# Softmax denominators of an attention and SwiGLU kernel: the reciprocal taken of 14 columns between two 32x32 block transposes, in place of 448 columns

## The chip, the core and the metric

The kernel runs on one core of one Trainium2 chip. A core has five engines that run side by side, each through its own list of instructions in order: TensorE (PE in the profile) for matmuls, VectorE (DVE), ScalarE (ACT), GpSimd (POOL), and SyncE (SP), whose queue issues the DMAs here. They wait for one another through semaphores. The time is device time in microseconds (us) of one launch. Before the change it is 1558.87 us, the median of 3 runs (1558.22 to 1562.27).

## The reference

The program is an attention block followed by a gated feed-forward block, all in float32.

- Attention, for 8 batches x 12 heads, 448 positions, head dimension 64: `q` and `k` are RMS-normalised along the head dimension and multiplied by gains; `scores = q k^T / 8`; `attn = exp(scores - max)`; `attn = attn / (sum(attn) + 1e-9)`; output `attn v`.
- The heads are put side by side to rows `x` of 8*448 = 3584 tokens x 768.
- Feed-forward: `x` is RMS-normalised and multiplied by a gain; `g = x w_gate`, `val = x w_val` (768 to 1536); `out = (g * sigmoid(g) * val) w_out` (1536 to 768).

The sum of `attn` over the keys is the softmax denominator; there is one for every batch, head and query position. Its reciprocal is what the change is about.

## The kernel before

**Tiling.** Attention works on pairs of heads: `NG` = 48 pairs `g`, six (`NPAIR`) for each of 8 sequences `b`. The scores of a pair are computed transposed, keys on the partitions and the 448 queries along the free axis, so `exp` (tile `e`, by ScalarE, lines 566 and 656) needs no transposing before it is multiplied by `v`. The value product of a pair is gathered in a PSUM bank `av` of 128 x 448: 64 rows for the head dimension of one head, 64 for the other. There is only one buffer of that kind (`ps_m`, tag "m"), which the transposes of q and k share; a new `av`, or such a transpose, waits until the last one was read. No maximum is subtracted: a bound on the gains is computed (line 1555), and a second routine, `any_scores`, takes over where it fails; with these inputs it isn't run.

**The denominators.** TensorE also multiplies `exp` by a matrix of ones 64 columns wide, so the sum over the keys lands in *all* 64 rows of a head: `den`, 128 x 448 in PSUM, has 64 equal rows for one head and 64 equal rows for the other. This saves a broadcast later. There are two ways to it:

- The first 7 pairs: `sums(g)` (line 592) sums with 12 matmuls (line 598), takes the reciprocal straight from PSUM into `rd` (line 601), and calls `weigh`.
- The other 41 pairs: GpSimd first adds the seven `e` tiles (`later_sums`, lines 701 and 706). Every second pair, `totals(g)` (line 676) takes two pairs at once: it sums with the ones (line 684), ScalarE copies the banks to `rd` (lines 688 and 691), VectorE takes the reciprocal in place (line 693) and `weigh` follows.

`weigh(g, ...)` (line 625) multiplies `av`, or a copy of it already in `x`, by `rd` on VectorE (line 630). Some steps later ScalarE squares the result (line 635, into the buffer of `rd`) and GpSimd adds the squares to `ss` (line 636), from which, once in a sequence, the RMS factor of the feed-forward is made (`rms_x`, line 713, and `norm_x`, line 724).

**Feed-forward.** Sequence 0 uses plain matmuls (line 1432), the others Strassen-like products (`quad`, line 1078, matmuls on line 1073; second projection on lines 1297 and 1365), whose sums VectorE makes. The feed-forward of a sequence is cut into items in a list `todo`; `fill` (line 1466) puts as many of them between the attention steps of the next sequence as their costs say.

**Weights.** The weights come as float64. `convert()` (line 872) turns them to float32 in 72 pieces, each over several turns: DMA in (line 821), two ScalarE passes (lines 834 and 835), three VectorE passes (`join`, lines 840, 841 and 842), and an integer add on GpSimd (line 882); then the piece is stored for later sequences (line 870). This goes on until about 285 us.

**Order.** The whole order of each engine's list is written out by hand: `manual_schedule` for all five engines, with `pe(fn)` as the step counter and `after(n, fn)` to put the rest of a job n steps later. So no engine can pass a waiting instruction: what stands behind it in its own list waits too. The pool `tmp`, which holds `rd` in two buffers, lies in SBUF.

Of the kernel before, what the change touches and what calls it, by code (L numbers as in the profile page):

```python
# [8 lines left out]
F32 = mybir.dt.float32  # L9
# [9 lines left out]
B, H, S, D = 8, 12, 448, 64  # L19
# [316 lines left out]
def safe_scores(  # L336
# [20 lines left out]
    nc = tc.nc  # L357

    def pool(name, bufs, **kw):
        return ctx.enter_context(tc.tile_pool(name=name, bufs=bufs, **kw))  # L360
# [4 lines left out]
    e_pool, tmp, y_pool, rest_pool = pool("c_e", 11), pool("c_tmp", 1), pool("c_y", 3), pool("c_rest", 2)  # L365
# [8 lines left out]
    st = {}  # L374
# [24 lines left out]
    def own(j):  # L399
        return slice(j * D, (j + 1) * D)  # L400

    def across(j):
        return own(1 - j)
# [180 lines left out]
    def values(g):  # L584

        vt, av = st["v", g], st["av", g]
        for c in range(NK):
            for j in range(2):
                nc.tensor.matmul(av[own(j), 0:S], lhsT=vt[:, j, c], rhs=st["e", g, c, j], start=False,
                                 stop=(c == NK - 1), skip_group_check=True)  # L590

    def sums(g):


        den = st.pop(("den", g))
        for c in range(NK):
            for j in range(2):
                nc.tensor.matmul(den[own(j), 0:S], lhsT=ones, rhs=st["e", g, c, j], start=False, stop=c == NK - 1,
                                 skip_group_check=True)
        rd = st["rd", g] = tmp.tile([128, S], F32, name="rd", tag="rd", bufs=2)  # L600
        nc.vector.reciprocal(rd, den[:, 0:S])
        weigh(g, *((1, 1) if g == NPAIR - 1 else (3,)))

    def x_of(g):
# [20 lines left out]
    def weigh(g, n, m=None):  # L625

        b, hp = divmod(g, NPAIR)
        rd, x = st.pop(("rd", g)), x_of(g)
        held = ("av", g) not in st
        nc.vector.tensor_tensor(x, x if held else st.pop(("av", g))[:, 0:S], rd, ALU.mult)  # L630
        ss, m = st["ss", b], n + 1 if m is None else m
        if hp == 0:
            after(n, lambda: nc.scalar.activation(ss, x, ACT.Square))
        else:
            after(n, lambda: nc.scalar.activation(rd, x, ACT.Square))  # L635
            after(m, lambda: (nc.gpsimd.tensor_tensor(ss, ss, rd, ALU.add), st.update({("summed", b): hp})))  # L636
        if not held:
            close(g)
# [37 lines left out]
    def totals(g):  # L676

        which = (g, g - 1) if g > NPAIR + 1 else (g,)
        den = {i: ps_s.tile([128, 512], F32, name="den", tag="s") for i in which[::-1]}
        for i in which:  # L680
            es = st.pop(("es", i))
            for j in range(2):
                to = j if i == g else 1 - j
                nc.tensor.matmul(den[i][own(to), 0:S], lhsT=ones[across(j)], rhs=es[across(j)], start=True, stop=True)  # L684
        for i in which[::-1]:
            rd = st["rd", i] = tmp.tile([128, S], F32, name="rd", tag="rd", bufs=2)
            if i == g:
                nc.scalar.copy(rd, den[i][:, 0:S])
            else:
                for j in range(2):  # L690
                    nc.scalar.copy(rd[own(j)], den[i][across(j), 0:S])  # L691
        for i in which[::-1]:
            nc.vector.reciprocal(st["rd", i], st["rd", i])  # L693
            if i < g:
                weigh(i, 3, 4)

# [381 lines left out]
    def quad(b, fp):  # L1078
# [72 lines left out]
        def p3_last():  # L1151
            if fp == NFP - 1 and in_quads(b):
                after(1, lambda: left_q1(b, 0, range(3)))
            p3()
            if fp % KG == KG - 1:
                after(3, lambda: sums(0))
                after(3 if fp == NFP - 1 else 5, lambda: sums(1))
# [434 lines left out]
    for g in range(NG + 1):  # L1592
# [24 lines left out]
        if g <= NPAIR:  # L1617
            pe(lambda: score(g, (0,)))
            squares(g + 2, 0)
            squares(g + 2, 1)  # L1620
            if g > 1:
                pe(lambda: turn(g + 1, 0))
                some_rests(g)
                pe(lambda: turn(g + 1, 1))
            pe(lambda: rests(g))
            pe(lambda: values(g - 1))
            if g == 1:
                pe(lambda: turn(g + 1, 0))
                some_rests(g)
                pe(lambda: turn(g + 1, 1))  # L1630
            load_v(g + 2)

            turns(1 if g == 1 else 3 if g < NPAIR else 0)
            pe(lambda: sums(g - 1))
            pe(lambda: score(g, (1, 2)))
            turns(2 if g == 1 else 3 if g == NPAIR else 0)
            if g == 2:
                bound()
            if g == NPAIR - 1:
                for half in range(2):  # L1640
                    norm_k(g + 2, half)
            continue

        if g == NPAIR + 1:
            some = lambda *parts: [exps(g, i, scores(g, i)) for i in parts]
            pe(lambda: (rests(g), some(0, 1)))
            pe(lambda: rms_x(0))
            pe(lambda: values(g - 1))
            load_v(g + 2)
            pe(lambda: some(2, 3))  # L1650
            pe(lambda: norm_x(0))
            pe(lambda: some(4, 5))
            pe(lambda: sums(g - 1))
            later_sums(g, 2)
            begin(0, 15)
        else:
            sums_due = g % 2 == 0
            pe(lambda: (totals(g - 1) if sums_due else None, step(g, 0)))
            pe(lambda: [step(g, i) for i in (1, 2)])
            load_v(g + 2)  # L1660
            pe(lambda: [step(g, i) for i in (3, 4)])
            pe(lambda: ([step(g, i) for i in (5, 6)], weigh(g - 1, 2) if sums_due else hold(g - 1)))
            if g < NG:
                later_sums(g, 2)
# [32 lines left out]
@with_exitstack  # L1697
def kernel(ctx: ExitStack, tc: tile.TileContext, *args):
    nc = tc.nc
    flag = ctx.enter_context(tc.tile_pool(name="flag", bufs=1)).tile([1, 1], I32, name="flag")  # L1700
    safe_scores(tc, *args, flag)
    large = nc.values_load(flag[0:1, 0:1], min_val=0, max_val=1)
    with tc.If(large > 0):
        any_scores(tc, *args)
# [28 lines left out]
```

## Time and profile before

| | before |
|---|---|
| median of 3 runs | 1558.87 us |
| the profiled execution | 1557.32 us |
| its span, first to last instruction | 1555.5 us |
| ScalarE busy | 535.3 us, 34% |
| GpSimd busy | 734.3 us, 47% |
| all DMA | 327 MB, mean 210 GB/s |
| mean granted TensorE clock | 0.994 |

How to read it: the profile is of one execution, whose time is 1.8 us more than its span. A row of a group names line, engine, operation, tiles written and read, partitions x elements, and the count; then total busy time, the mean of one in ns, and the idle time of the engine ahead of it. A row of the timeline gives start, length, engine, line, operation, tiles and count, and in brackets the engine's idle time ahead and what ended it. TensorE's matmuls are pipelined and their ends are modelled, so it counts as busy even where it gets through less than it could.

### The profile page before, as it was taken

Reading aid. Unit: us, or ns where it says so; the run is one execution under the profiler, and the core shown is the slowest. Engines: PE = TensorE matmul, PEld = TensorE weight load, DVE = VectorE, ACT = ScalarE, POOL = GpSimd, SP = SyncE. Lnnn points to the kernel's source line nnn. Section 1 sums busy time; section 2 is a strip of 40 time slices with the busy share of each in tenths; the row PEclk is TensorE's granted clock in tenths of the full one; section 3 lists DMA queues with packets and bytes.
Section 4 is the critical chain, followed back from the end, with each engine's and each line's share of the span. In section 5 each row is a group of like instructions: output and inputs, shape, how many; then the busy total and the mean of one; then the engine's idle time right before and its main releaser. Section 6 shows DMA issues by size and latency. Waiting matters only on the chain.

```text
span 1555.5 us, 25996 instructions
## 1 busy us (share of the span) xinstructions
PE 1515.4 (97%) x8900; PEld 1187.2 (76%) x8900; DVE 1009.3 (65%) x1697; ACT 535.3 (34%) x1241; POOL 734.3 (47%) x718
## 2 busy tenths in 40 slices
PE   8999998999999999999999999999999999999997
PEld 4344444687855888878987889768888789899997
DVE  6889989668864677855468564643568554673454
ACT  6756654433323333233333242333432332101000
POOL 6868877556433354463535644444544732021003
PEclk9999999999999999999999999999999999999999
DMA  7657565676889987986557765485557755578665
GB/s 205 210 154 242 185 207 164 208 237 213 285 268 288 316 259 230 281 257 187 166 157 229 236 196 165 139 260 161 159 148 234 227 172 147 156 263 255 174 195 180
DMA packets 314081, 327.26 MB, mean 210 GB/s; under 512 B 84308, under 2 KB 310868, under 8 KB 313940
## 3 DMA queue, kind: packets, MB, share of 16 engines
q1 hardware_dynamic: 313012, 325.31, 68.2%
q8 instruction: 73, 1.20, 0.3%
q14 instruction: 68, 0.56, 0.1%
q10 hardware_dynamic: 800, 0.20, 0.1%
q0 software_dynamic: 128, 0.00, 0.0%
HBM read 271.62 MB, written 53.77 MB: 209 GB/s over the span
## 4 chain that ended last, share of the span: by engine, by line
PE 80%; DVE 14%; issue 2%; DMA 2%; POOL 1%; ACT 1%; SPq 1%; DVEq 0%; POOLq 0%; ACTq 0%
PE ff L1073 41%; PE ff L1365 10%; PE sc L651 7%; PE av L666 5%; PE ff L1297 5%; PE ff L1432 4%; DVE rd L693 2%; PE tr L544 2%; PE ff L1170 2%; DVE top L842 1%; DVE top L841 1%; PE den L684 1%; DVE l L1240 1%; DVE top L840 1%; DVE ms L496 1%
## 5 line engine op out<-in xcount | busy, mean ns | idle before, releaser
L1073 PE MATMUL ff<-x,w 128*128 128x224 f32 x1686 | 344.4, 354 | 0.0
L1073 PEld LDWEIGHTS ff<-x,w 128*128 128x128 f32 x1686 | 315.2, 190 | 13.2 <-issue 10.6
L1073 PE MATMUL ff<-xs,w 128*128 128x224 f32 x1296 | 265.4, 353 | 4.9 <-DVE cc L1085 3.7
L706 POOL TENSOR_TENSOR es<-es,e 128x448 f32<-128x448 f32 x205 | 243.5, 1188 | 13.7
L1073 PEld LDWEIGHTS ff<-xs,w 128*128 128x128 f32 x1296 | 243.8, 190 | 6.8 <-DVE cc L1085 4.6
L651 PE MATMUL sc<-qT,kT 64*64 64x448 f32 x1176 | 233.9, 542 | 4.5 <-ACT e L656 3.1
L666 PE MATMUL av<-e,vt 64*64 64x448 f32 x984 | 194.4, 541 | 0.0
L656 ACT ACTIVATE e<-sc 128x448 f32<-128x448 f32 x294 | 154.7, 546 | 70.5 <-PE sc L651 52.5
L636 POOL TENSOR_TENSOR ss<-ss,rd 128x448 f32<-128x448 f32 x40 | 47.3, 1182 | 249.2 <-ACT rd L635 249.2
L651 PEld LDWEIGHTS sc<-qT,kT 64*64 64x64 f32 x1176 | 79.2, 133 | 85.9 <-issue 58.8
L693 DVE RECIPROCAL rd<-rd 128x448 f32<-128x448 f32 x41 | 120.8, 2947 | 24.9 <-ACT rd L691 24.8
L701 POOL TENSOR_TENSOR es<-e 128x448 f32<-128x448 f32 x41 | 49.8, 1215 | 165.0 <-ACT e L656 165.0
L515 POOL TENSOR_TENSOR rs<-ms,mhalf 128x12 f32<-128x12 f32 (+1 forms) x50 | 116.1, 2322 | 4.2
L1085 DVE TENSOR_TENSOR cc<-ff,u 128x448 f32<-128x448 f32 x84 | 52.4, 623 | 97.9 <-PE ff L1073 97.8
L1432 PE MATMUL ff<-x,w 128*128 128x448 f32 x288 | 113.3, 547 | 0.0
L1365 PE MATMUL ff<-w,l 128*128 128x192 f32 x500 | 96.6, 331 | 3.4 <-DVE l L1240 2.0
L666 PEld LDWEIGHTS av<-e,vt 64*64 64x64 f32 x984 | 66.4, 133 | 42.4 <-issue 42.4
L1092 ACT ACTIVATE th<-c 128x224 f32<-128x224 f32 x42 | 16.3, 389 | 237.5 <-DVE c L1085 237.5
L1432 PEld LDWEIGHTS ff<-x,w 128*128 128x128 f32 x288 | 54.0, 193 | 52.3 <-issue 50.9
L1365 PEld LDWEIGHTS ff<-w,l 128*128 128x128 f32 x500 | 82.3, 190 | 10.2 <-DVE l L1240 3.8
L1337 POOL TENSOR_TENSOR y<-y,c 128x384 f32<-128x384 f32 x10 | 12.1, 1215 | 159.5 <-DVE y L1406 148.0
L1085 DVE TENSOR_TENSOR u<-ff,u 128x448 f32<-128x448 f32 x42 | 26.1, 622 | 77.6 <-PE ff L1073 77.0
(207 smaller groups left out, 2611.3 us busy)
## 6 DMA issues: line engine op xcount, KB each, us to landing
w<-kept SPq DMA_DIRECT2D x474, 192.0 KB, 3.7
w<-kept_q SPq DMA_DIRECT2D x297, 192.0 KB, 3.7
w<-kept_o SPq DMA_DIRECT2D x132, 192.0 KB, 3.9
kept<-w SPq DMA_DIRECT2D x81, 192.0 KB, 3.9
top<-kept SPq DMA_DIRECT2D x78, 192.0 KB, 4.0
top<-kept_q SPq DMA_DIRECT2D x53, 192.0 KB, 3.5
kept_q<-w SPq DMA_DIRECT2D x52, 192.0 KB, 2.8
qk<-in_q_dram SPq DMA_DIRECT2D x48, 192.0 KB, 3.5
```

The lines of the kernel that those rows point to most:

```text
L515: nc.gpsimd.tensor_tensor(st["rs", g][:, cols], ms, mhalf[:, cols], ALU.pow)
L651: nc.tensor.matmul(ps[r, 0:S], lhsT=st["kT", g][r, keys_of(i)], rhs=st["qT", g][r, :], start=True, stop=True)
L656: nc.scalar.activation(e, ps[:, 0:S], ACT.Exp)
L666: nc.tensor.matmul(st["av", g][own(j), 0:S], lhsT=vt, rhs=st["e", g, i][r], start=i == 0, stop=i == PARTS - 1, skip_group_check=True)
L693: nc.vector.reciprocal(st["rd", i], st["rd", i])
L701: nc.gpsimd.tensor_tensor(st["es", g], st["e", g, 0], st["e", g, 1], ALU.add)
L706: nc.gpsimd.tensor_tensor(st["es", g], st["es", g], st["e", g, i], ALU.add)
L1073: nc.tensor.matmul(bank[:, w * HT:(w + 1) * HT], lhsT=wt[:, c * 128:(c + 1) * 128], rhs=x[:, c, :], start=onto is None and w == c == 0, st ...
L1085: nc.vector.tensor_tensor(add[name], ps[:, 0:S], add[other], ALU.add)
L1297: nc.tensor.matmul(ps, lhsT=left_o(b, which, LEFT_O[name], c), rhs=data(("wo", b, name, c)), start=first and c == 0, stop=c == NFP - 1, sk ...
L1365: nc.tensor.matmul(ps, lhsT=a[:, j, :], rhs=data(key)[:, n % 2 * HW:(n % 2 + 1) * HW], start=start and j == 0, stop=j == KG - 1, skip_grou ...
L1432: nc.tensor.matmul(bank[w][:, 0:S], lhsT=data(key)[:, c * 128:(c + 1) * 128], rhs=st["x", 0, half][:, c, :], start=half == c == 0, stop=ha ...
```

## The change

Both reciprocals, on lines 601 and 693, are replaced by a function `invert(rd, den)`, which runs three VectorE instructions:

1. `den` (448 columns, seen as 14 blocks of 32) is transposed in blocks of 32 x 32 into `rd`. The rows of a block are equal, so after it every *column* of a block is the same: row p of block n holds the denominator of query 32n + p, 32 times over.
2. The reciprocal of the first column of each block, 14 elements in a row, goes to a new small tile `few` (128 x 14, one buffer in `tmp`).
3. `few`, each element repeated 32 times by a stride of zero, is transposed in blocks of 32 x 32 into `rd`, which then has in all rows the reciprocals of all 448 queries, as before.

Rows 0 to 63 and 64 to 127 belong to two heads; a 32-row block lies wholly in one of them.

```diff
+    def invert(rd, den):
+
+        few = tmp.tile([128, S // 32], F32, name="few", tag="few", bufs=1)
+        squares_of = lambda t: t.rearrange("p (n c) -> p n c", c=32)
+        nc.vector.transpose(out=squares_of(rd), in_=squares_of(den))
+        nc.vector.reciprocal(few, squares_of(rd)[:, :, 0])
+        nc.vector.transpose(out=squares_of(rd), in_=few.unsqueeze(2).to_broadcast([128, S // 32, 32]))
+
     def sums(g):
...
         rd = st["rd", g] = tmp.tile([128, S], F32, name="rd", tag="rd", bufs=2)
-        nc.vector.reciprocal(rd, den[:, 0:S])
+        invert(rd, den[:, 0:S])
...
         for i in which[::-1]:
-            nc.vector.reciprocal(st["rd", i], st["rd", i])
+            invert(st["rd", i], st["rd", i])
```

## The prediction

> **What bounds the kernel now.** I read the page first: its busy shares, then the slices.
>
> ```profile
> PE 1515.4 (97%) x8900; PEld 1187.2 (76%) x8900; DVE 1009.3 (65%) x1697; ACT 535.3 (34%) x1241; POOL 734.3 (47%) x718
> DVE  6889989668864677855468564643568554673454
> ```
>
> TensorE is busy 97% of the span, and VectorE 65%. So what VectorE saves is not time saved as such: it counts only where TensorE stands still for VectorE. The slices (39 us each) say where that may be: VectorE is at 8 or 9 tenths in slices 2 to 6 (39 to 273 us), while the weights are converted, and rarely later. The second view is busy time by stretches, which I cut at the marks of these stages (columns: stretch and length, busy us and instructions of PE, PEld, DVE, ACT, POOL, granted clock, DMA share, GB/s):
>
> ```profile
> 0.00:100.00 100.00, 90.13 (x471) 38.74 (x472) 72.61 (x127) 67.85 (x141) 72.67 (x84) 1.00 0.70 203
> 100.00:168.00 68.00, 68.00 (x281) 33.38 (x280) 64.57 (x97) 42.52 (x99) 54.99 (x51) 1.00 0.63 194
> 168.00:272.00 104.00, 94.18 (x443) 45.51 (x442) 94.95 (x128) 56.62 (x128) 78.86 (x74) 0.95 0.62 189
> 272.00:1555.50 1283.50, 1263.09 (x7708) 1069.61 (x7707) 777.13 (x1346) 368.28 (x875) 527.82 (x511) 1.00 0.69 214
> ```
>
> TensorE idles 9.9 us before 100 us, 0 from 100 to 168, 9.8 from 168 to 272, and 20.4 in the whole rest, where VectorE is only 61% busy. From 168 to 272 VectorE is busy 91% and the granted clock falls to 0.95. The third view is TensorE's timeline, for the places where it idles (the brackets give the idle time and what ended it):
>
> ```profile
> 43.62 0.97 PE L576 MATMUL av<-e,vr 64*64 64x448 f32 x4 [1.70 <-DVE row L1552]
> 87.04 0.59 PE L576 MATMUL av<-e,vr 64*64 64x448 f32 x2 [1.20 <-issue]
> 182.18 0.52 PE L544 MATMUL tr<-ident,qn 128*128 128x128 f32 x3 [0.81 <-DVE x L630]
> 203.12 0.71 PE L651 MATMUL sc<-qT,kT 64*64 64x448 f32 x2 [3.06 <-ACT e L656]
> 203.61 0.96 PE L651 MATMUL sc<-qT,kT 64*64 64x448 f32 x2
> 204.36 0.96 PE L651 MATMUL sc<-qT,kT 64*64 64x448 f32 x2
> 242.77 0.95 PE L718 MATMUL msx<-ones,ss 128*112 128x1 f32 x8 [0.64 <-POOL ss L636]
> 247.63 0.90 PE L544 MATMUL tr<-ident,qk 128*128 128x128 f32 x3 [3.91 <-DVE kT L550]
> ```
>
> Each of these but the later ones (after 272) stands behind a reciprocal. VectorE's own timeline ahead of 182.18 shows how:
>
> ```profile
> 174.84 2.94 DVE L693 RECIPROCAL rd<-rd 128x448 f32<-128x448 f32 x1
> 177.82 0.62 DVE L630 TENSOR_TENSOR x<-x,rd 128x448 f32<-128x448 f32 x1
> 178.36 2.94 DVE L693 RECIPROCAL rd<-rd 128x448 f32<-128x448 f32 x1
> 181.41 0.62 DVE L630 TENSOR_TENSOR x<-av,rd 128x448 f32<-128x448 f32 x1
> ```
>
> The second product frees the one `av` bank at 182.03, and the transpose of `qn`, which wants that bank, starts at 182.18.
>
> **The change, part by part.** It removes 48 reciprocals (41 on line 693, 7 on line 601) and puts in 96 block transposes and 48 short reciprocals, in the same place of VectorE's list. No DMA and no other engine's instruction is added or moved. Groups of VectorE by shape give the prices:
>
> ```profile
> L693 DVE RECIPROCAL rd<-rd 128x448 f32<-128x448 f32 x41 | 120.8, 2947 | 24.9 <-ACT rd L691 24.8
> L601 DVE RECIPROCAL rd<-den 128x448 f32<-128x448 f32 x7 | 20.6, 2950 | 3.3 <-POOL rs L515 2.8 <-PE den L598 0.5
> L630 DVE TENSOR_TENSOR x<-av,rd 128x448 f32<-128x448 f32 x28 | 17.4, 621 | 1.2
> L550 DVE COPY kT<-tr 128x64 f32<-128x64 f32 x48 | 10.6, 221 | 43.5 <-ACT qT L549 43.5
> ```
>
> *Fixed cost and cost per element.* Line 630 takes 621 ns for 448 columns, the copy on line 550 221 ns for 64: (621 - 221)/384 = 1.04 ns a column and 221 - 64*1.04 = 154 ns fixed. A reciprocal from SBUF or PSUM alike takes 2.95 us, so (2947 - 154)/448 = 6.2 ns a column.
>
> *The short reciprocal:* 154 + 14*6.2 = 241 ns. The columns lie 32 apart; I take no extra for it, at most another 0.1 us.
>
> *A transpose.* The trace has no VectorE transpose. From below: VectorE's fastest pass over SBUF here, line 841 when GpSimd is quiet, takes 0.36 us for 384 columns, so 0.4 us. Near: one column a cycle, as line 630, 0.62 us. From above: two columns' time each, 154 + 448*2.08 = 1.09 us, or more, for an unknown form; four would be 2.0 us, and the reciprocal shows that VectorE has operations at six. A price is stated by the Trainium skill, "VectorE: DVE Perf Modes", section "The three transpose paths": 311 ns for 128 columns of 16-bit data. Less 154 fixed that is 1.2 ns a column, and for 448 an estimate of 154 + 448*1.2 = 0.70 us if 32-bit columns go as fast, which the page doesn't say. I take 0.65 us, between row and page, keep 0.4 and 2.0 as ends.
>
> *The waits between the three.* Each needs the result of the one before. In the trace a dependent VectorE instruction starts 0.04 us after the end (177.78 to 177.82); two of them are 0.08.
>
> *Sum for one call:* 0.65 + 0.04 + 0.24 + 0.04 + 0.65 = 1.62 us against 2.95: **1.33 us saved**, 48*1.33 = 64 us of VectorE's 1009. On line 601 `den` is also free 2.3 us earlier, since the first transpose is its last reader; TensorE isn't seen waiting for that bank.
>
> **A rule that speaks against it.** From 201.87, beside GpSimd's line 882, line 841 takes 1.05 us, against 0.36 alone: two engines share a way to SBUF. The Trainium skill, "GPSIMD Engine Reference", section "1. Specifications", says so: they contend where VectorE runs in a two-port mode or reads two SBUF inputs. By the line-841 rows a transpose under contention would cost about 1.05*448/384 = 1.2 us, one call 2.75, and nearly nothing is saved. But the rule leaves one-port operations out, and the row agrees: all 41 reciprocals took 2939 to 2954 ns with GpSimd at 47%. Whether a transpose is a one-port operation no row here shows; the page "Vector Engine (DVE) Microarchitecture Reference", section "5.1 Performance modes", lists only copy, cast and tensor_scalar for the two-port mode. So I take it uncontended.
>
> **Where the 1.33 us counts.** Place by place, with each shift stopped where VectorE meets the next input that isn't earlier.
>
> - *43.62 us.* VectorE runs without a break from 22.9 to 43.6 with two reciprocals (26.60, 39.87), and TensorE idles 1.70. The saving, 2.66, covers it: **1.7**; 1.3 if only the second call counts.
> - *65.5 us.* The reciprocal at 61.76 ends in the product that frees `av`; TensorE shows no idle time but starts its next matmul late by half a microsecond: **0.3**.
> - *83 to 95 us.* The reciprocal at 83.32 starts as soon as its `den` is there. TensorE waits for its product (1.20), then for `ss` (0.46), then for the RMS factor at 94.97 (0.72); the last hangs on VectorE too, without a break since 83.32. The chain moves as a whole: **1.3**.
> - *168 to 207 us.* Two reciprocals, 2.66 us off VectorE's list. The 0.81 at 182.18 goes. The 3.06 at 203.12 is a longer chain: ScalarE stands 6.05 us on line 834 for a buffer that GpSimd frees on line 882. GpSimd is busy without a break from 184.50, where it waited for VectorE, to 203.8. Its list ahead of 184.50 (`ss`, one piece, two `es`, 1.1 us each, from 179.19) can itself move only about 2.2, so the chain moves **2.2** in all, the 0.81 among it.
> - *The clock there.* After the 3.06 us of idling, pairs of matmuls start 0.75 us apart from 203.61 to 206.60, and 0.37 before 199.5: half clock, 5 steps * 0.37 = 1.9 us lost. Idle times of 1.70 and 1.20 had no such effect. With 3.06 cut to about 1.7, the half clock should not come: **1.9**.
> - *214 to 252 us.* Two reciprocals (230.83, 234.35), and TensorE idles 0.64 + 3.91. But behind them VectorE's line 1443 at 243.45 needs matmuls that end at 242.14, so VectorE gains at most 1.3 there: **1.3**. Over 3 us of idling stay, and the half clock from 244.4 to 251.2, seen as a matmul group of 18 that takes 8.4 us in place of 6.9, with it.
> - *After 272 us.* 36 calls, 48 us of VectorE, **0**: what covers them is TensorE's queue of feed-forward matmuls. At 350.26, for one, VectorE had idled 1.86 us before the reciprocal, and after the second product it idles 0.64 and 1.65 us waiting for line 1073. The four larger waits there (367.5, 426.2, 557.1 and 621.0) each come after VectorE had met TensorE again. What is gained is idle time of VectorE.
>
> Sum: 1.7 + 0.3 + 1.3 + 2.2 + 1.9 + 1.3 = **8.7 us**. Against the profiled execution's 1557.3 this gives 1548.6; that execution lies 1.5 under the median of the runs shown, so on their scale 1558.9 - 8.7 = **1550.2**, say 1550.
>
> **The rivals.**
>
> 1. *Hidden after all.* The gain in the conversion stage goes to GpSimd's or the DMA's chain: the 203.12 wait isn't shortened beyond the 0.81, and the half clock stays. For it: at 203 the chain runs through GpSimd, 79 of 104 us busy, and loads wait there too (205.89 to 210.22). Against: VectorE starts that chain. Then 1.7 + 0.3 + 1.3 + 0.8 + 0.6 (half of the last place) = 4.7 or less, 1554 to 1558. The same comes of transposes at 1.1 to 1.3 us.
> 2. *More than that.* VectorE isn't stopped at line 1443, the second half clock goes too (8.4 - 6.9 = 1.5), and the wait at 557.06 (1.3) goes: 8.7 + 1.4 + 1.5 + 1.3 = 13, 1546. For it: GpSimd's collisions with VectorE change with the order, and lines 840 to 842 take 0.56 to 1.4 us by them. Against: they can as well fall worse.
> 3. *Slower.* A 32-bit transpose runs at a fraction of a column a cycle. It decides from (2.95 - 0.24 - 0.08)/2 = 1.31 us on. At 2.0 us a call costs 4.3, 1.4 more than before; at each place above, with no slack on VectorE, that is on the path: 2.8 + 1.4 + 1.4 + 2.8 + 2.8 = 11 us, 1570; nothing after 272, where the idle times of VectorE take it. For it: no row shows this operation. Against: the page's 1.2 ns a column, for 16-bit data.
>
> That the change doesn't do what it says, splitting a transpose into many instructions, is part of the third.
>
> **How the numbers follow.** The forecast has 0.50, hidden 0.20, more 0.15, slower 0.15. A kernel of this kind can be told from no change at about 0.3%, 4.7 us. Faster: 0.50 + 0.15 = 0.65. Same: the hidden case, 0.20. Slower: 0.15. The range goes from 1543, under the second rival by its uncertain collisions, to 1562, over the hidden case and the gentle end of the slow one; about 0.05 lies below and 0.12 above. The likeliest alone, with 1.3 for the first place and without one of the smaller terms, or with one more: 1546 to 1554.
>
> **What would show it.** The group of transposes: 96 at 0.62 to 0.72 us, with a narrow spread even beside GpSimd; 48 reciprocals at 0.24; VectorE about 945 us busy. TensorE: no idle time near 43 us, under 2 us near 200 and no half clock there, still over 2.5 near 245. If the 203 wait keeps its length behind line 882, the chain through GpSimd was not VectorE's. Transposes over 1.3 us, or spread from 0.65 to 1.3, would make the prediction wrong at the first step; and new waits of TensorE after 272 us at the last.

## The result and the profile after

The changed kernel takes **1544.87 us** (median of 4 runs, 1544.02 to 1546.19) against 1559.91 us for the kernel before (median of 4, 1558.22 to 1562.27): ratio 0.9903, 95% interval 0.9886 to 0.9920. So it is faster by 15.0 us, or 1.0%. The forecast was 1550 in a range of 1543 to 1562: right in direction and inside the range, but below the 1546 to 1554 that was called likeliest alone, and the gain is 1.7 times the 8.7 us summed up. The profiled executions lie closer together, 1557.32 and 1546.19 us: the one before is faster than each of the four runs, the one after is the slowest of its four.

The page after, its busy shares and VectorE's slices:

```profile
PE 1511.2 (98%) x8900; PEld 1187.4 (77%) x8900; DVE 929.8 (60%) x1793; ACT 534.8 (35%) x1241; POOL 736.4 (48%) x718
DVE  5788998667754666854457443444458444673464
```

VectorE is busy 79.5 us less, TensorE's matmuls are the same 8900. The groups by shape give the new operations their price (line numbers after line 589 are 8 higher than before):

```profile
L598 DVE STREAM_TRANSPOSE rd<-few 128x448 f32<-128x448 f32 x48 | 31.0, 645 | 1.6
L596 DVE STREAM_TRANSPOSE rd<-rd 128x448 f32<-128x448 f32 x41 | 26.2, 640 | 25.1 <-ACT rd L699 25.0
L597 DVE RECIPROCAL few<-rd 128x14 f32<-128x14 f32 x48 | 11.6, 242 | 1.6
L596 DVE STREAM_TRANSPOSE rd<-den 128x448 f32<-128x448 f32 x7 | 4.5, 641 | 3.3 <-POOL rs L515 2.8 <-PE den L606 0.5
```

A transpose takes 0.64 us and a short reciprocal 0.242: a call is 1.6 us, as assumed. The list of operations on `rd` gives the spread: line 598 645 to 647 ns, line 596 630 to 650. By the trace, 23 of the 96 transposes run for most of their time beside one of GpSimd's tensor_tensor operations, and they take 630 to 649 ns; the 60 with none beside them take 635 to 650. So GpSimd is not seen to slow them. What replaces 141.4 us of reciprocals is 73.3 us; the other 11 us that VectorE is less busy come from operations that the change doesn't touch. This is the part that the prediction lacked.

By stretches (the same cuts as before; the work has moved forward by up to 12 us):

```profile
0.00:100.00 100.00, 92.76 (x478) 41.05 (x479) 66.87 (x144) 67.59 (x141) 72.75 (x84) 1.00 0.72 209
100.00:168.00 68.00, 68.00 (x282) 33.08 (x280) 61.76 (x99) 43.21 (x100) 57.43 (x53) 1.00 0.62 192
168.00:272.00 104.00, 95.16 (x457) 46.61 (x457) 92.83 (x137) 60.01 (x138) 79.97 (x74) 0.98 0.61 190
272.00:1544.40 1272.40, 1255.25 (x7688) 1066.70 (x7686) 708.30 (x1415) 364.02 (x864) 526.25 (x508) 1.00 0.69 215
```

And TensorE's timeline at the places that were forecast:

```profile
43.30 0.97 PE L576 MATMUL av<-e,vr 64*64 64x448 f32 x4
84.38 0.59 PE L576 MATMUL av<-e,vr 64*64 64x448 f32 x2
178.78 0.49 PE L544 MATMUL tr<-ident,qn 128*128 128x128 f32 x3
199.35 0.59 PE L659 MATMUL sc<-qT,kT 64*64 64x448 f32 x2 [2.93 <-ACT e L664]
236.51 0.86 PE L726 MATMUL msx<-ones,ss 128*112 128x1 f32 x8
240.53 0.55 PE L544 MATMUL tr<-ident,qk 128*128 128x128 f32 x3 [3.17 <-DVE kT L550]
261.14 0.59 PE L659 MATMUL sc<-qT,kT 64*64 64x448 f32 x2 [2.74 <-DVE x L744]
```

The brackets at 43, 87, 182 and 242 us are gone. Those at 203 and 247 are there still, at 199.35 and 240.53. The last row, at 261.14, had a shorter wait before:

```profile
268.62 0.59 PE L651 MATMUL sc<-qT,kT 64*64 64x448 f32 x2 [1.35 <-DVE x L736]
```

TensorE runs the same matmuls in the same order, so the start of the n-th one can be compared between two traces; the growth of that difference is the gain at a place.

| place (us, before) | forecast | gain in the traces |
|---|---|---|
| start (warming matmuls) | none | -1.4 |
| 43 | 1.7 | 1.7 |
| 65 | 0.3 | 1.0 |
| 83 to 95 | 1.3 | 1.1 |
| 182 and 203, waits | 2.2 | 1.4 |
| 203 to 207, half clock | 1.9 | 1.6 |
| 242 and 247, waits | 1.3 | 1.6 |
| 247 to 252, half clock | 0 | 1.8 |
| 268 to 272 | 0 | -3.1 |
| after 272 | 0 | 6.2 |
| sum, at the last matmul | 8.7 | 12.0 |

The first row is the execution, not the change: in the trace of before TensorE comes to full clock in the first microseconds, in that of after it runs its warming matmuls 1.4 us longer. Two things ask for an explanation: 6.2 us after 272 us, where nothing was expected; and the waits at 203 and 247 that hardly shrank.

### The profile page after: what moved, and what is told of

It reads as the page before. It is cut to its first block, busy times and chain, and to the rows that moved or that the text cites. A ratio compares the mean times of both kernels' runs of the same rounds, so it can differ in the third digit from the quotient of the medians.

```text
span 1544.4 us, 26111 instructions
## 1 busy us (share of the span) xinstructions
PE 1511.2 (98%) x8900; PEld 1187.4 (77%) x8900; DVE 929.8 (60%) x1793; ACT 534.8 (35%) x1241; POOL 736.4 (48%) x718
## 4 chain that ended last, share of the span: by engine, by line
PE 83%; DVE 11%; DMA 2%; issue 1%; ACT 1%; POOL 1%; SPq 0%; DVEq 0%; POOLq 0%; ACTq 0%
PE ff L1081 42%; PE ff L1373 10%; PE sc L659 7%; PE av L674 6%; PE ff L1305 5%; PE ff L1440 4%; PE tr L544 2%; PE ff L1178 2%; DVE top L850 1%; DVE top L849 1%; PE den L692 1%; PE den L606 1%; DVE top L848 1%; PE sc L562 1%; DVE l L1248 1%
## 5 line engine op out<-in xcount | busy, mean ns | idle before, releaser
L1100 ACT ACTIVATE th<-c 128x224 f32<-128x224 f32 x42 | 16.3, 389 | 238.1 <-DVE c L1093 238.1
L1093 DVE TENSOR_TENSOR u<-ff,p 128x448 f32<-128x448 f32 x42 | 26.2, 623 | 84.3 <-PE ff L1081 77.9
```

The source lines that it names most:

```text
L1093: nc.vector.tensor_tensor(add[name], ps[:, 0:S], add[other], ALU.add)
```

## Experiments

Two theories. **Q**, the prediction's: what counts is the length of VectorE's own list, where it is behind. **C**: VectorE and GpSimd slow each other where VectorE's two-input operations run beside GpSimd's additions; the short call moves them apart after 272 us. Each run was timed against the kernel before on the same chip.

**Where the gain is.** The function for the pairs up to 11, or from 12 on, alone:

```diff
     def invert(rd, den, g):
+        if not (g < 12):        # second run: g >= 12
+            nc.vector.reciprocal(rd, den)
+            return
```

> The new function for pairs 0 to 11 alone (before 272 us); pairs 12 to 47 keep the reciprocal of 448 columns. Theory Q (on record: what counts is VectorE's own list, and after 272 us it has slack): all of the gain is here, 1544 to 1546 us. Theory C (after 272 us the earlier product lets GpSimd's adds run ahead of VectorE's two-input operations, so that they collide less): the traces' 5.8 us up to 272 us, perhaps 9 by the medians, so 1550 to 1554 us.

> The new function for pairs 12 to 47 alone; the first 12 keep the reciprocal of 448 columns. Theory Q: nothing, 1558 to 1561 us. Theory C: about 6 us less than before, 1552 to 1555 us, with the gain at the waits near 426, 557 and 621 us of the trace of before.

The first takes 1552.73 us against 1560.57, ratio 0.9950 (0.9935 to 0.9965), 7.8 us gained; the second 1554.02, ratio 0.9956 (0.9942 to 0.9970), 6.5 us. The sum, 14.4, is the whole within its uncertainty. Nearly half of the gain thus lies where VectorE is only 61% busy. Theory Q, as put on record, fails here.

**Is it VectorE's time?** A reciprocal of 190 columns (1342 ns) fills the call up to its old length:

```diff
         nc.vector.reciprocal(few, squares_of(rd)[:, :, 0])
+        nc.vector.reciprocal(rd[:, 0:190], rd[:, 0:190])
         nc.vector.transpose(out=squares_of(rd), in_=few...)
```

> A reciprocal of 190 columns (about 1.33 us) is put in ahead of the second transpose, its result is overwritten: VectorE is occupied as long as before the change, and the product comes as late as before. Both theories: the whole gain goes, 1558 to 1561 us. If it stays below 1555 us, something else than VectorE's time counts (the PSUM bank of the denominators, free earlier, or the form of the operation).

1561.53 us, ratio 1.0007 (0.9998 to 1.0017): the whole gain is gone. Neither the earlier release of the PSUM bank nor the form of the operation counts. This kernel thus also gives a second trace at the speed of before (profiled execution 1561.50 us). Against it, the changed kernel's last matmul starts 16.3 us earlier, 8.1 of them after 272 us. This is nearer to the medians than the first trace of before.

**List or product?** The same time, spent after the product:

```diff
         nc.vector.tensor_tensor(x, x if held else ..., rd, ALU.mult)
+        for _ in range(5):
+            nc.vector.reciprocal(st["few"], st["few"])
```

> The same time (five short reciprocals in place, about 1.4 us) is spent on VectorE after the product that uses the reciprocals: its list is as long as before, but the product comes early. Theory Q (length of the list): nearly all of the gain goes, 1557 to 1561 us. Theory C: what comes after 272 us stays, and so do the places where TensorE waits for the product itself (43, 65, 87 and 182 us); lost are the places further down VectorE's list: 1548 to 1553 us.

1552.99 us, ratio 0.9948 (0.9935 to 0.9962), half of the gain. The number is the one that C named, but not for the reason it gave. Matmul by matmul against the trace with the filler ahead, 4.9 us are won by 272 us, most at 45, 67 and 88 us, where TensorE waits for the product itself, and only 1.7 after 272. But this run does not hold the product apart from the list as well as was meant: where two pairs are done in turn, the filler of the first stands ahead of the second call, and the second product comes hardly earlier than before. Near 426 us it ends 10.1 us after the first call began, against 10.6 before and 6.2 in the changed kernel. So the run shows that the saved time must be free on VectorE's list; it does not test an early second product.

Group rows of operations that no version changes show what it loses: the two steps behind the gate of the feed-forward (lines 1095 and 1096 before; two SBUF inputs), busy us and mean ns. The kernel before:

```profile
L1095 DVE SCALAR_TENSOR_TENSOR h<-th,cc 128x448 f32<-128x448 f32 x42 | 33.9, 806 | 0.7 <-ACT th L1092 0.7
L1096 DVE SCALAR_TENSOR_TENSOR h<-h,cc 128x448 f32<-128x448 f32 x42 | 28.1, 669 | 1.4
L1096 DVE SCALAR_TENSOR_TENSOR h<-h,c 128x224 f32<-128x224 f32 x42 | 23.7, 565 | 1.5
```

The same groups of the changed kernel:

```profile
L1103 DVE SCALAR_TENSOR_TENSOR h<-th,cc 128x448 f32<-128x448 f32 x42 | 26.4, 629 | 0.7 <-ACT th L1100 0.7
L1104 DVE SCALAR_TENSOR_TENSOR h<-h,cc 128x448 f32<-128x448 f32 x42 | 27.1, 645 | 1.4
L1104 DVE SCALAR_TENSOR_TENSOR h<-h,c 128x224 f32<-128x224 f32 x42 | 17.3, 411 | 1.5
```

And with the filler after the product:

```profile
L1105 DVE SCALAR_TENSOR_TENSOR h<-th,cc 128x448 f32<-128x448 f32 x42 | 33.9, 806 | 0.7 <-ACT th L1102 0.7
L1106 DVE SCALAR_TENSOR_TENSOR h<-h,cc 128x448 f32<-128x448 f32 x42 | 34.6, 824 | 1.4
L1106 DVE SCALAR_TENSOR_TENSOR h<-h,c 128x224 f32<-128x224 f32 x42 | 24.7, 589 | 1.4
```

The changed kernel does the same work in 15 us less (70.8 for 85.7), and with the filler after the product it takes 93.2, longer than before. The timeline shows the mechanism. VectorE before, around the wait of TensorE at 426 us:

```profile
412.51 0.33 DVE L1095 SCALAR_TENSOR_TENSOR h<-th,c 128x224 f32<-128x224 f32 x1
412.88 1.21 DVE L1096 SCALAR_TENSOR_TENSOR h<-h,c 128x224 f32<-128x224 f32 x1
414.00 1.55 DVE L1095 SCALAR_TENSOR_TENSOR h<-th,cc 128x448 f32<-128x448 f32 x1
...
420.42 3.69 DVE L1016 TENSOR_TENSOR w<-w,w 128x384 f32<-128x384 f32 x3
```

GpSimd before, the same stretch:

```profile
412.42 1.42 POOL L701 TENSOR_TENSOR es<-e 128x448 f32<-128x448 f32 x1
413.91 1.16 POOL L706 TENSOR_TENSOR es<-es,e 128x448 f32<-128x448 f32 x1
417.44 1.14 POOL L636 TENSOR_TENSOR ss<-ss,rd 128x448 f32<-128x448 f32 x1 [2.37 <-ACT rd L635]
418.53 5.17 POOL L706 TENSOR_TENSOR es<-es,e 128x448 f32<-128x448 f32 x4
```

The second reciprocal pushes lines 1095 and 1096 into the time of GpSimd's additions, and they take 2.5 to 3 times as long as in the changed kernel (1.21 and 1.55 us for 0.39 and 0.61). They make the second product late; GpSimd waits 2.37 us for it (`ss`), with four additions queued behind, and those then run beside line 1016, whose three take 3.69. Changed kernel, VectorE:

```profile
404.44 0.39 DVE L1104 SCALAR_TENSOR_TENSOR h<-h,c 128x224 f32<-128x224 f32 x1
404.75 0.61 DVE L1103 SCALAR_TENSOR_TENSOR h<-th,cc 128x448 f32<-128x448 f32 x1
...
414.11 0.62 DVE L1093 TENSOR_TENSOR u<-ff,u 128x448 f32<-128x448 f32 x1 [0.66 <-PE ff L1081]
414.65 2.09 DVE L1024 TENSOR_TENSOR w<-w,w 128x384 f32<-128x384 f32 x3
```

and GpSimd:

```profile
405.56 1.46 POOL L644 TENSOR_TENSOR ss<-ss,rd 128x448 f32<-128x448 f32 x1 [12.09 <-ACT rd L643]
...
409.27 1.13 POOL L644 TENSOR_TENSOR ss<-ss,rd 128x448 f32<-128x448 f32 x1
410.36 4.78 POOL L714 TENSOR_TENSOR es<-es,e 128x448 f32<-128x448 f32 x4
```

Now VectorE is nearly past the gate when GpSimd begins, the second `ss` does not wait, and the additions end before most of line 1024. The row at 414.11 settles what is won here: VectorE stands still for TensorE, so the time saved on the reciprocals is used up. What counts from there on is that line 1024 takes 1.6 us less; TensorE gains 0.96. The waits at 557 and 621 us end likewise. Behind an idle time of VectorE in the changed kernel, lines 1043 to 1045 take 0.52 and 1.84 us less than before, and TensorE gains 0.53 and 1.84.

The other places after 272 us are of another kind, and come three times alike, near 673, 861 and 1214 us. Before, VectorE runs from the reciprocal through the product to line 1397 without a break, and TensorE waits for it:

```profile
668.96 2.94 DVE L693 RECIPROCAL rd<-rd 128x448 f32<-128x448 f32 x1
672.00 0.62 DVE L630 TENSOR_TENSOR x<-av,rd 128x448 f32<-128x448 f32 x1
672.54 0.55 DVE L1397 TENSOR_TENSOR y<-ff,th 128x384 f32<-128x384 f32 x1
673.15 2.30 PE L1365 MATMUL ff<-w,l 128*128 128x192 f32 x12 [0.26 <-DVE y L1397]
```

In the changed kernel VectorE waits for TensorE there:

```profile
661.93 0.56 DVE L1405 TENSOR_TENSOR y<-ff,th 128x384 f32<-128x384 f32 x1 [0.97 <-PE ff L1373]
```

This gives 0.61 us each time and needs no collision. Another 0.35 comes some 10 us later each time, where line 1240 beside the additions takes 0.89 us in place of 1.24. So of the 6.2 us after 272, the traces put 1.8 to VectorE's shorter list and 4.4 to collisions.

Added up over the trace, all VectorE instructions other than reciprocals and transposes take 732.1 us after 272 us before the change and 712.9 after it; 739.4 with the filler after the product, 732.5 with the filler ahead of it.

**The additions taken away.** If collisions are the cause, the late gain should shrink where GpSimd has less to add:

```diff
     def later_sums(g, n):
...
         after(n, first)
+        if g >= 12:
+            return
         after(n + 2, lambda: more(3, 4))
         after(n + 3, lambda: more(5, 6))
```

> The kernel before, but for pairs 12 to 47 GpSimd adds only the first three of the seven exp tiles (four additions a pair are left out, so their denominators are not complete). Reciprocals as before. Theory C (after 272 us VectorE is late for TensorE because its two-input operations run beside GpSimd's adds): the late part of the gain, about 6 us, comes without any change of the reciprocal: 1552 to 1556 us. Theory Q (only the length of VectorE's own list counts): within 1 us of before, 1559 to 1562 us.

> The changed kernel with the same four additions a pair left out. Theory C: nothing more to gain after 272 us, so 1543 to 1546 us, and its distance to the kernel before without the additions is the early part alone, about 8 to 9 us. Theory Q: the same time as the changed kernel, but a distance of 14 to 16 us.

Before, without the additions: 1547.83 us against 1560.42, ratio 0.9916 (0.9901 to 0.9931), 12.6 us faster with no reciprocal touched, twice what C expected. After, without them: 1536.94, ratio 0.9850 (0.9836 to 0.9863), where C had expected no further gain. So the additions cost both kernels time, 12.6 and about 8 us. The distance between the two is 10.9 us in place of 15.0. Their two traces put it: 9.8 us are there at the matmul of 268 us, and only 1.9 come after, against 8.1 with the additions (the changed kernel against the filler ahead of the transpose). The 1.9 are the three places of line 1397, 0.61 us each; at 426, 557 and 621 us there is next to nothing (0.1 in sum). So about three quarters of the late gain hang on these additions, and the rest is VectorE's own list.

**The additions moved.** In the same pairs all six additions stand ahead of the second `ss` in GpSimd's list:

```diff
-        after(n + 2, lambda: more(3, 4))
-        after(n + 3, lambda: more(5, 6))
+        after(n if g >= 12 else n + 2, lambda: more(3, 4))
+        after(n if g >= 12 else n + 3, lambda: more(5, 6))
```

> The kernel before; for pairs 12 to 47 GpSimd's additions of exp tiles stand in its list ahead of the second sum of squares, so they don't wait for the late product. No work is left out. Theory C: a part of the late gain, as GpSimd's run starts 2 to 3 us earlier and meets fewer of VectorE's operations: 1555 to 1558 us. Theory Q: 1559 to 1562 us.

> The same order of GpSimd's additions in the changed kernel, where the product is early already. Theory C: next to nothing, 1543 to 1546 us; it would show a gain only where GpSimd still waits for a product. Theory Q: the same as the changed kernel, 1544 to 1546 us.

Both miss: 1565.29 us, ratio 1.0032 (1.0020 to 1.0044), and 1554.34, ratio 0.9960 (0.9947 to 0.9974), some 5 and 9 us slower than their counterparts. Neither theory had this. In the first, the list of TensorE's operations on line 718, the row sums for the RMS factor, names a longer wait (total us and times, weight loads and matmuls both counted):

```profile
  POOL ss L636: 24.1, 14
```

Before, the same entry is

```profile
  POOL ss L636: 3.7, 4
```

By TensorE's matmuls alone these are 7 waits of 10.4 us in sum, against 2 of 1.1 before. VectorE's other instructions did fall, from 732.1 to 722.0 us after 272, as C says. But what was moved behind the additions is `ss`, and once in a sequence TensorE stands behind it. A wait took the place of the collisions, so these two runs measure an order and do not test the theory.

## Why the prediction came out as it did

- **The price of a call** held: 1.6 us for 1.62. Both doubts about the transpose are settled, by 630 to 650 ns over 96 of them, those beside GpSimd's work included. The rule of the Trainium skill that was weighed ("GPSIMD Engine Reference", section "1. Specifications") was rightly left out for the transposes. The third rival, a slow transpose, falls by this.
- **43, 65 and 83 to 95 us**: right, 3.8 for 3.3. At the first two and at 87 us TensorE waits for the product itself, and the filler after the product left most of these gains in place.
- **168 to 207 us**: 3.0 for 4.1. The waits gave 1.4 in place of 2.2, and 2.93 us of idling remain, not 1.7. The step that failed is the assumption that VectorE's other instructions keep their length. Behind the second product, before:

```profile
181.95 0.65 DVE L840 TENSOR_SCALAR top<-top 128x384 f32<-128x384 f32 x1
182.63 1.19 DVE L841 TENSOR_SCALAR top<-top 128x384 int32<-128x384 int32 x1
183.86 0.56 DVE L842 SCALAR_TENSOR_TENSOR top<-raw,top 128x384 int32<-128x384 int32 x1
```

  and after:

```profile
176.82 1.21 DVE L848 TENSOR_SCALAR top<-top 128x384 f32<-128x384 f32 x1
178.06 1.18 DVE L849 TENSOR_SCALAR top<-top 128x384 int32<-128x384 int32 x1
179.28 1.38 DVE L850 SCALAR_TENSOR_TENSOR top<-raw,top 128x384 int32<-128x384 int32 x1
```

  GpSimd begins its run at 175.71, on the heels of the first product, and now meets all three: of 2.66 us saved, 1.4 are lost again. Over the whole stage these other instructions grew from 210.3 to 215.1 us. Here the collisions work against the change.
- **The half clock near 203** did go, but not for the reason given, so this part came right by luck: 2.93 us of idling are hardly less than 3.06. The stretch from 190 to 215 us before and after (the clock is the third number from the end):

```profile
190.00:215.00 25.00, 21.88 (x98) 10.32 (x97) 19.69 (x31) 14.37 (x34) 22.80 (x21) 0.93 0.59 181
```

```profile
190.00:215.00 25.00, 22.07 (x105) 10.32 (x104) 22.66 (x31) 13.91 (x33) 23.08 (x22) 1.00 0.74 234
```

  In this stretch it is 0.93 in all six traces with a long list there (waits of 3.06 to 3.07 us), and 1.00 in all four with the short one (2.93 to 2.98). Why 0.1 us should decide is not settled, and the length of the wait alone does not decide. Near 245 us a wait of 3.2 went without half clock in the changed kernel and with it where only the early pairs were changed.
- **214 to 252 us**: 1.6 for 1.3 in the waits, and a half clock of 1.8 us that was to stay was absent in this trace. Then **268 us**: what TensorE had gained ahead of VectorE it gave back. VectorE is without a break from 208.8 to 261.1 and sets the time; the wait grew from 1.35 to 2.74, and after it a half clock came that was not there before.
- **After 272 us**: "0" is the step that failed most, in two ways. Its argument, that VectorE meets TensorE again before each of the four larger waits, held for the queue at 367, 426 and 621 us. But a waiting place of TensorE behind VectorE need not be moved by the queue alone: when the call ends, GpSimd's run starts, and which of VectorE's operations that run meets decides whether they take 0.4 or 1.2 us. That gave 4.4 us. And the argument looked at the larger waits only: at the small ones of line 1365, near 673, 861 and 1214 us, VectorE had no slack behind the reciprocal, which gave 1.8. The second rival had named such shifts, for one wait and 1.3 us, with the remark that they could as well fall worse. Both happened: worse before 272 us, better after.
- **Readings that were off**: VectorE's 8 and 9 tenths are in slices 2 to 7, not 2 to 6, and none of TensorE's rows shown there is later than 272 us. Ahead of 557 us VectorE had idled for only 0.13 us since the second product. None of this changes a sum.

So direction and range were right, and the size came from another place than stated for nearly half of the gain. The runs count it as 7.8 us early and 6.5 late. No run took the collisions away in the early stage, so what they cost there is read from the traces alone.

## What to carry to other kernels

Equal rows on the partitions are worth a look: a costly function of a value held in 32 equal rows can be taken once for 32 columns, and the two block transposes and the short reciprocal cost 1.6 us against 2.95 for a reciprocal of 448 columns here. When an engine gets shorter work, look at its small waits as well as its large ones, and don't only ask who waits for it; ask which operations of its neighbour now run at the same time as which of its own, since a two-input VectorE operation next to GpSimd's additions took two to three times as long. And before work is moved out of a collision, look for who waits for what is moved behind it.

## What was not expected of the hardware

- VectorE's block transpose of 448 float32 columns, from SBUF or from PSUM, or from 14 columns repeated by a stride of zero, takes 0.64 us, about as long as a product of the same size (0.62), and GpSimd's additions don't lengthen it (630 to 649 ns beside them). The reciprocal takes 6.2 ns a column, 242 ns for 14.
- Two-input operations and the tensor_scalar on SBUF do get longer beside GpSimd: the two-input step of 128 x 224 from 0.39 to 1.21 us, the tensor_scalar of 128 x 384 from 0.36 to between 1.05 and 1.19.
- Leaving out four of GpSimd's six additions a pair, on an engine that was idle half the time, made the kernel before 12.6 us faster: nearly as much as the change itself.
